# Interleaving the stages of neighbouring channel groups in an FFT convolution that feeds a token-mixing layer

## The chip, the cores and the metric

The kernel runs on one core of one Trainium2 chip. The metric is the device time of one execution in microseconds (us). The kernel before took 2565.59 us (median of 2 runs, 2563.41 to 2567.76). Runs and profiled executions are not the same thing. Times of stages come from one profiled execution of each kernel, whose span is within about 6 us of the median of its runs.

Names of engines in the profile: PE is TensorE (matmuls), PEld its weight loads, which overlap the matmuls (busy 2141.6 and 1267.6 us of a span of 2569.7), DVE is VectorE, ACT is ScalarE, POOL is GpSimd, SP is SyncE, which here only issues transfers. A letter q after an engine (ACTq, SPq) marks the transfers which that engine issues. PSUM is the memory into which this kernel's matmuls write, and VectorE or ScalarE copy the results out of it. The weights of a matmul are the operand whose load the profile shows as an instruction of its own, LDWEIGHTS (stage A of the kernel before has 1280 of them for 1280 matmuls).

## The reference

Two layers in a row. The first convolves each of 128 channels of `x` along the sequence with a filter `h`, by Fourier transforms of twice the length. The second mixes the tokens with two 5696 x 5696 matrices.

```python
x: (8, 5696, 128)    h: (5696, 128)
def _attn_ref(x, h):
    L = 2 * S                                     # 11392
    Yf = np.fft.rfft(x, n=L, axis=1) * np.fft.rfft(h, n=L, axis=0)[None]
    return np.fft.irfft(Yf, n=L, axis=1)[:, :S, :]

def _moe_ref(x, w_theta, w_tok_r, w_tok_i, w_ch):  # x is the convolution's output
    theta = x @ w_theta
    zr, zi = x * np.cos(theta), x * np.sin(theta)
    y = einsum('ts,bsd->btd', w_tok_r, zr) + einsum('ts,bsd->btd', w_tok_i, zi)
    u = x + y
    return u + np.maximum(u @ w_ch, 0.0)
```

## The kernel before

The kernel has four parts, one after another in time: a setup (tables of sines, the spectrum of `h`), the convolution in eight groups (four pairs of batches times two halves of 64 channels), a middle part that loads the convolution's output `yt_hbm`, transposes it into tiles of 128 tokens and forms cosine and sine, and the token mixing.

The transform of length 11392 is split into 178 x 64, and of the 178 row frequencies the 90 from 0 to 89 are computed, in two halves of 45 (`KH`). One group consists of four stages, which I call A, B, C and D.

```python
# A, row transforms: 8 chunks of 8 matmuls for each frequency half
def f1(x16, d0, kh, m):
    a_ = fa.tile([P, 2 * KH, HD], F16, tag="a", name="a_")
    lhs = x16.rearrange("p b n d -> p (b n) d")
    for q in range(0, HD, 8):
        ps = psum()
        for i in range(8):
            nc.tensor.matmul(ps[:m, ...], lhs[:NB, :m, d0 + q + i],      # weights: columns 128 elements apart
                             f1_t[:NB, kh]..., start=True, stop=True)
        nc.scalar.activation(a_[:m, :, q:q + 8]..., ps[:m, ...], AF.Copy)
    return a_
...
for bp in range(B // 2):
    x16 = load_x(lambda e: x[2 * bp + e], 2)
    for dh in range(2):
        for kh in range(2):
            a_ = f1(x16, dh * HD, kh, P)
            for c, (c0, ck) in enumerate(CHK):       # B: 6 chunks per half
                hs = fh.tile([P, 2, HD * CK], F16, tag="hs", name="hs")     # 3 buffers
                nc.sync.dma_start(hs, hf_hbm[dh, kh * NCK + c])
                ps = f2(a_, kh, c, 2)
                xs = fs.tile(...)
                nc.scalar.activation(xs..., ps..., AF.Copy)
                k0 = kh * KH + c0
                for r in range(2):                   # the product with the spectrum
                    nc.vector.tensor_tensor(uv[r][:, :, :, k0:k0 + ck], xs..., hv..., op=mult)
        for q in range(0, 2 * HD, 8):                # C: 16 chunks of 16 matmuls
            ps = psum()
            for i in range(8):
                nc.tensor.matmul(o, u_t[:, at:at + P], r_u, start=True, stop=False)
                nc.tensor.matmul(o, v_t[:, at:at + P], r_v, start=False, stop=True)
            # copied out of PSUM by VectorE for a third of the chunks, by ScalarE for the others
        for n0, cn in CHN:                           # D: 7 chunks
            et = fs.tile([P, CN, 2, NB], F16, tag="et", name="et")          # 2 buffers
            nc.sync.dma_start(et[:K1, :cn], e_hbm[:, n0:n0 + cn, :, :])
            ... matmuls on g_ and et ...
            nc.vector.tensor_copy(yt[...], ps[...])
        for e in range(2):
            nc.sync.dma_start(yt_hbm[dh * HD:(dh + 1) * HD, 2 * bp + e, :], yt[...])
```

In the middle part, ScalarE issues the loads of `ya` in 17 pieces, and all 45 token tiles are transposed and stored there, though the mixing needs only the first 22 at its start.

```python
for p_ in [0, 1, 2, 4, 5, 6, 3, 7] + list(range(8, len(pieces))):        # 17 pieces
    nc.scalar.dma_start(ya[:, :, t0:t1], yt_hbm[:, :, t0:t1])
...
        y_ap = rows_of(ti)            # transpose, copy, store: a tile that is needed now
        phases_b(ti, y_ap, ...)       # its cosine and sine
        if rest:
            rows_of(rest.pop())       # and one of the late tiles 22..44
```

## Time and profile before

The time of the profiled execution (span 2569.7 us) falls into these parts. The bounds are the first matmul of stage C, the issue of the last store of `yt_hbm`, and the first matmul of the mixing.

| part | from – to (us) | length |
|---|---|---|
| setup, and A and B of the first group | 0 – 164.2 | 164.2 |
| groups, from the first C to the last D | 164.2 – 738.8 | 574.6 |
| middle | 738.8 – 907.6 | 168.8 |
| mixing | 907.6 – 2569.7 | 1662.1 |

The head of the page of the kernel before gives the busy time of each engine over the whole span, with its share and number of instructions. Two rows of its part with 40 slices follow (each about 64 us; tenths of the slice in which TensorE was busy, and tenths of full clock that TensorE was granted).

```profile
span 2569.7 us, 42694 instructions
PE 2141.6 (83%) x16395; PEld 1267.6 (49%) x16567; DVE 1729.4 (67%) x2942; ACT 728.2 (28%) x988; POOL 814.1 (32%) x1507
PE   4375776757645569999999999979999999999998
PEclk9975666666668679999999999999999999999998
```

The 83% is an average of two different programs. Counted from zero, the slices from 15 on show TensorE nearly full at full clock (one of them has a 7). In slices 3 to 11, where the groups run, it is busy for four to seven tenths, at a clock of five to six tenths. The views of windows show the same by part. Each line gives the window, its length, busy time and number of instructions for PE, PEld, DVE, ACT and POOL, then the mean granted clock, the busy share of the transfer engines and GB/s. (The profile counts a packet whole in the window in which it starts, so a share can come out a little above 1.) The lines are the setup, one whole group (432 to 504), the middle, and the mixing once it is at its pace.

```profile
core 0: us, PE busy (x) PEld busy (x) DVE busy (x) ACT busy (x) POOL busy (x), PEclk, DMA share, GB/s
0.00:164.20 164.20, 76.36 (x1104) 74.76 (x1105) 88.77 (x105) 92.93 (x124) 18.03 (x31) 0.93 0.42 104
432.00:504.00 72.00, 51.65 (x879) 50.16 (x880) 40.74 (x37) 34.43 (x39) 0.00 (x0) 0.67 0.35 94
738.80:907.60 168.80, 79.13 (x788) 61.95 (x800) 81.88 (x111) 89.69 (x110) 0.00 (x0) 0.70 0.84 234
977.00:2570.00 1593.00, 1549.74 (x7815) 734.94 (x7969) 1212.12 (x2368) 270.73 (x446) 759.80 (x1408) 0.99 0.83 149
```

In the group of 72 us no engine is busy for more than 52 us, and the transfers take a third of their time. The stages mostly follow one another, each with another limit. The trace of the same group shows that the first products (from 443.57 us) wait 10.20 us for ScalarE, which copies stage A out as TensorE delivers it. It also shows two durations for one product of the same shape, 0.69 us in the first frequency half and about 1.3 us in the second. The columns are start, duration, engine, line, operation, operands, and in brackets the idle time before it with what ended it.

```profile
443.57 0.69 DVE L255 TENSOR_TENSOR u_t<-xs,hs 128x1024 f16<-128x1024 f16 x1 [10.20 <-ACT xs L250]
460.41 1.28 DVE L255 TENSOR_TENSOR u_t<-xs,hs 128x1024 f16<-128x1024 f16 x1 [2.08 <-ACT xs L250]
```

In the middle part, the trace of ScalarE shows it issuing 17 loads for 35.22 us before its first copy of a transposed tile at 782.34 us.

```profile
747.07 35.22 ACTq L416 DMA_DIRECT2D ya<-yt_hbm  x17
782.34 0.60 ACT L429 ACTIVATE y_ap<-tpz 128x512 bf16<-128x512 bf16 x1 [64.22 <-issue]
```

The page's part with the costliest groups of instructions gives the two lines that the argument returns to: all products into `u_t` (96 of them, the mean of the two durations), and the weight loads of stage A, which the profile books at 263 ns each.

```profile
L255 DVE TENSOR_TENSOR u_t<-xs,hs 128x1024 f16<-128x1024 f16 x96 | 127.8, 1332 | 130.0 <-ACT xs L250 95.3
L189 PEld LDWEIGHTS <-x 89*128 89x128 f16 (+1 forms) x1280 | 157.3, 263 | 78.4 <-issue 64.9
```

The mean of 1332 ns in the first line is above both 0.69 and 1.3 us. The reason is a third kind of product. The kernel before computes stage A of the second half beside stage B of the first, and there some products take longer still, like this one, while TensorE runs matmuls of A:

```profile
450.02 3.37 DVE L255 TENSOR_TENSOR v_t<-xs,hs 128x1024 f16<-128x1024 f16 x1
450.36 3.05 PE L189 MATMUL ps<-f_t,x 89*128 89x90 f16 x24 [1.23 <-ACT xs L250]
```

Sorted by this overlap, the trace is clear. Of the 80 products of this shape in the first halves, the 38 that ran beside matmuls of A for 0.3 us or more took 1.05 to 4.55 us, and all but one of the others 0.66 to 0.72 (that one overlapped for 0.23 us and took 0.73). ScalarE's copies of A don't do it: the 8 smaller products (128x640) of these halves that ran beside such copies and beside no matmul of A took 0.84 to 0.91 us (those of the second halves, beside neither, 0.89 to 0.94), and those beside matmuls of A 1.17 to 2.70. GpSimd is not busy in the group shown (0.00 us).

So the order of a group in the kernel before is A0, B0 with A1 beside it, B1, C, D.

### The profile page before, as it was taken

The page shows a single profiled execution, that of the slowest core. Times are in us where ns is not written, and L with a number is a line of the kernel's source. Part 1 is how long each engine was busy: PE and PEld are TensorE (multiplying, and loading weights), DVE is VectorE, ACT ScalarE, POOL GpSimd, SP SyncE. Part 2 cuts the span into 40 slices and gives each one's busy share as a digit, 9 for nine tenths or more (in the row PEclk, how much of TensorE's full clock was granted, in tenths as well). Part 3 has the DMA queues.
Part 4 walks back from the last instruction along what each step waited for, and adds up shares of the span by engine and source line. Part 5 has one row for each costly group of instructions (what it writes and reads, how often), then busy time and mean ns, then how long its engine had stood idle before and what let it go on. Part 6 is the DMA issues. An engine that isn't in the chain of part 4 may idle for free.

```text
span 2569.7 us, 42694 instructions
## 1 busy us (share of the span) xinstructions
PE 2141.6 (83%) x16395; PEld 1267.6 (49%) x16567; DVE 1729.4 (67%) x2942; ACT 728.2 (28%) x988; POOL 814.1 (32%) x1507
## 2 busy tenths in 40 slices
PE   4375776757645569999999999979999999999998
PEld 4365676657634434444444444433444444444444
DVE  6355554555514668888878876769777777777774
ACT  6454453445417622333323310000111111111111
POOL 1000000000020014445554565534445544454441
PEclk9975666666668679999999999999999999999998
DMA  1725344343388778889978999897788877888773
GB/s 34 178 82 131 105 108 108 97 103 99 93 190 231 220 219 160 164 166 168 159 142 158 162 163 151 136 260 125 137 140 153 142 138 136 140 153 137 141 134 67
DMA packets 399093, 367.99 MB, mean 143 GB/s; under 512 B 58400, under 2 KB 340170, under 8 KB 397062
## 3 DMA queue, kind: packets, MB, share of 16 engines
q0 software_dynamic: 218240, 143.00, 41.4%
q1 hardware_dynamic: 156951, 197.86, 26.4%
q10 hardware_dynamic: 23696, 24.38, 3.1%
q8 instruction: 130, 2.13, 0.3%
q14 instruction: 76, 0.62, 0.1%
HBM read 404.85 MB, written 103.12 MB: 198 GB/s over the span
## 4 chain that ended last, share of the span: by engine, by line
PE 61%; DMA 10%; DVE 6%; issue 4%; ACT 3%; POOL 1%; ACTq 1%; SPq 0%; DVEq 0%; POOLq 0%
PE m L741 49%; DMA et<-e_hbm 2%; PE ps L265 2%; PE ps L264 2%; DVE v_t L255 2%; DMA hs<-hf_hbm 2%; PE ps L189 2%; DMA y_hbm<-y_ap 2%; DMA wb<-in_moe_w_tok_r_dram 1%; ACTq L416 1%; POOL wb L466 1%; PE ps L281 1%; DVE c L748 1%; DVE u_t L255 1%; DMA wb<-in_moe_w_tok_i_dram 1%
## 5 line engine op out<-in xcount | busy, mean ns | idle before, releaser
L466 POOL DMA_DIRECT2D wb<-in_moe_w_tok_i_dram x720 | 387.8, 547 | 899.0 <-DVE wt L475 809.3
L466 POOL DMA_DIRECT2D wb<-in_moe_w_tok_r_dram x720 | 386.7, 548 | 296.5 <-ACT g__9038 L271 186.8
L741 PE MATMUL m<-b,wt 128*128 128x512 bf16 x1891 | 451.3, 382 | 20.8 <-DVE b L391 9.8
L475 DVE STREAM_TRANSPOSE wt<-wb 128x384 f32<-128x384 f32 (+2 forms) x720 | 359.9, 524 | 125.1 <-PE m L741 69.4
L741 PEld LDWEIGHTS <-wt 128*128 128x128 bf16 x1936 | 190.0, 98 | 252.0 <-issue 20.2
L748 DVE TENSOR_TENSOR c<-c,m 128x512 f32<-128x512 f32 x440 | 283.6, 669 | 0.0
L557 ACT ACTIVATE uts<-utp 128x512 bf16<-128x512 bf16 (+1 forms) x90 | 53.3, 592 | 615.9 <-PE utp L555 615.9
L264 PE MATMUL ps<-r_u,u_t 128*128 128x128 f16 x1024 | 133.3, 235 | 111.7 <-DVE u_t L255 111.7
L189 PE MATMUL ps<-f_t,x 89*128 89x90 f16 (+1 forms) x1280 | 160.7, 324 | 76.5 <-ACT xs L250 18.6
L255 DVE TENSOR_TENSOR u_t<-xs,hs 128x1024 f16<-128x1024 f16 x96 | 127.8, 1332 | 130.0 <-ACT xs L250 95.3
L189 PEld LDWEIGHTS <-x 89*128 89x128 f16 (+1 forms) x1280 | 157.3, 263 | 78.4 <-issue 64.9
L264 PEld LDWEIGHTS <-u_t 128*128 128x128 f16 x1024 | 107.5, 106 | 112.9 <-DVE u_t L255 112.9
L250 ACT ACTIVATE xs<-ps 128x1024 f16<-128x1024 f32 x96 | 108.8, 1151 | 113.9 <-DVE v_t L255 88.0
L108 POOL DMA_DIRECT2D x<-in_x_dram x16 | 8.6, 544 | 407.5 <-PE ps L189 407.5
L265 PE MATMUL ps<-r_v,v_t 128*128 128x128 f16 x1024 | 129.6, 234 | 0.8
L255 DVE TENSOR_TENSOR v_t<-xs,hs 128x1024 f16<-128x1024 f16 x96 | 122.4, 1275 | 0.0
L552 ACT ACTIVATE ub<-c 128x512 bf16<-128x512 f32 (+1 forms) x90 | 56.5, 628 | 222.3 <-DMA wb<-in_moe_w_tok_i_dram 158.6
L206 PEld LDWEIGHTS <-w_t 64*128 64x128 f16 x3240 | 96.4, 126 | 32.0 <-issue 29.8
L283 DVE CAST yt<-ps 128x890 bf16<-128x890 f32 (+1 forms) x56 | 55.5, 1004 | 80.5 <-PE ps L281 80.2
L265 PEld LDWEIGHTS <-v_t 128*128 128x128 f16 x1024 | 107.8, 106 | 2.9 <-DVE v_t L255 2.9
L423 PE MATMUL tpz<-ident_bf,ya 128*128 128x128 bf16 (+1 forms) x360 | 34.8, 260 | 68.5 <-DMA ya<-yt_hbm 39.5
L309 ACT ACTIVATE yT<-tpz 128x512 bf16<-128x512 bf16 x46 | 27.1, 590 | 179.5 <-PE tpz L305 179.5
(2851 smaller groups left out, 3830.6 us busy)
## 6 DMA issues: line engine op xcount, KB each, us to landing
wb<-in_moe_w_tok_r_dram POOLq DMA_DIRECT2D x352, 96.0 KB, 4.5
wb<-in_moe_w_tok_i_dram POOLq DMA_DIRECT2D x352, 96.0 KB, 4.8
wb<-in_moe_w_tok_r_dram POOLq DMA_DIRECT2D x352, 80.0 KB, 4.5
wb<-in_moe_w_tok_i_dram POOLq DMA_DIRECT2D x352, 80.0 KB, 3.7
hs<-hf_hbm SPq DMA_DIRECT2D x96, 256.0 KB, 2.6
cp_hbm<-c SPq DMA_DIRECT2D x88, 256.0 KB, 2.4
c<-cp_hbm SPq DMA_DIRECT2D x88, 256.0 KB, 4.4
out_dram<-c SPq DMA_DIRECT2D x88, 256.0 KB, 4.2
```

What stands on the lines that cost most here:

```text
L189: nc.tensor.matmul(ps[:m, i // 4, (i % 4) * 2 * KH:(i % 4 + 1) * 2 * KH], lhs[:NB, :m, d0 + q + i], f1_t[:NB, kh].rearrange("p r k -> p (r ...
L206: nc.tensor.matmul(ps[:, e, j * HD:(j + 1) * HD], w_t2[rows, k1, N2 * (1 - ri):N2 * (3 - ri)], a_[rows, ri * KH + c0 + j, :], start=(ri == ...
L250: nc.scalar.activation(xs[:, :, :, :ck], ps[:, :, :ck * HD].rearrange("p e (k d) -> p e d k", k=ck), AF.Copy)
L255: nc.vector.tensor_tensor(uv[r][:, :, :, k0:k0 + ck], xs[:, :, :, :ck], hv[:, r:r + 1, :, :ck].to_broadcast([P, 2, HD, ck]), op=mult)
L264: nc.tensor.matmul(o, u_t[:, at:at + P], r_u, start=True, stop=False)
L265: nc.tensor.matmul(o, v_t[:, at:at + P], r_v, start=False, stop=True)
L283: nc.vector.tensor_copy(yt[:, :, n0:n0 + cn].rearrange("p m (a q) -> p m a q", q=nq), ps[:, :cn // nq, :nq * NB].rearrange("p a (q m) -> p ...
L466: nc.gpsimd.dma_start(wb[32 * i:32 * i + 32, :ng, :nj * 64], bass.AP(tensor=a.tensor, offset=a.offset + row0 * S + p * H + i * QR + j0 * 6 ...
L475: nc.vector.transpose(wt.rearrange("p j t r -> p (j t r)").bitcast(F32).rearrange("p (j g t) -> p g j t", j=TJ, g=4)[:, :ng, :nj], wb[:, : ...
L552: nc.scalar.activation(ub[:m].rearrange("p b d -> p (b d)"), c[:m], AF.Copy)
L741: nc.tensor.matmul(ms[q], a[q][:, j, :, r], bts[jj][q][:, r, :], start=(jj == 0 and r == 0), stop=(jj == NJ - 1 and r == 1 and q not in left))
L748: nc.vector.tensor_tensor(c, z, ms[q], op=op)
```

## The change

The change has four parts, meant to fill the idle engines of the first three parts of the span. It leaves the arithmetic of the mixing alone.

1. **Order.** Each stage becomes a list of steps. Stage C of a group is put in program order between the steps of stage A of the next group, and stage D between those of the next stage B.
2. **Even halves.** The 90 frequencies are split into 46 and 44 instead of 45 and 45, so that the second half starts at an even column. All copies of stage C out of PSUM go to VectorE, those of D to ScalarE.
3. **Setup.** The spectrum of `h` is computed for both channel halves in one pass, with both halves of the array's rows in use, and stored in 16 transfers at its end. A chunk of the tables takes two sines and a change of sign instead of three sines. `h` has a buffer of its own, so that the first `x` is loaded at the start.
4. **Late tiles.** The middle loads and transposes only the 22 tiles that the mixing needs first (8 loads instead of 17). The 23 late tiles are loaded, transposed and stored during the mixing, among work of that kind that was there before. With it, the mixing loads some addends later than before.

```diff
+    HALF = ((0, K1 // 2 + 1), (K1 // 2 + 1, K1 // 2 - 1))
...
-        h16 = load_x(lambda e: h, 1)
+        x16s = {0: load_x(0)}
...
-        for dh in range(2):
-            for kh in range(2):
-                a_ = f1(h16, dh * HD, kh, 64)
-                for c, (c0, ck) in enumerate(CHK):
-                    ps = f2(a_, kh, c, 1)
-                    nc.scalar.activation(hst[:, kh * NCK + c, :, :ck], ps[...], AF.Copy, scale=16.0 / NF)
-            ... stores of this half
+        for kh in range(2):
+            for step in stage_a(lambda q: h16[...][:, :, q], kh, a_h):
+                step()
+        for c, (kh, c0, ck) in enumerate(CHK):
+            ps = f2(a_h, c)
+            ... copied by VectorE and ScalarE in turn
+        for dh in range(2):
+            for kh in range(2):
+                for ri in range(2):
+                    for e in range(2):
+                        (nc.sync if e else nc.scalar).dma_start(hf_hbm[dh, ...], hst[kh][...])
...
-                    if q % 24 == 8:
-                        nc.vector.tensor_copy(g_out, g_in)
-                    else:
-                        nc.scalar.activation(g_out, g_in, AF.Copy)
+                nc.vector.tensor_copy(st["g"][...], ps[...])
...
+        def woven(*lists):
+            steps = [((i + 0.5) / len(l), n, f) for n, l in enumerate(lists) for i, f in enumerate(l)]
+            for _, _, f in sorted(steps, key=lambda s: s[:2]):
+                f()
...
+        a0, a_of = front(0)
+        woven(a0)
+        woven(stage_b(a_of, 0))
+        setup.close()
+        for g, (bp, dh) in enumerate(groups):
+            st = {}
+            nxt, a_of = front(g + 1) if g + 1 < len(groups) else ([], None)
+            woven(stage_c(st), nxt)
+            if dh == 0 and bp + 1 < B // 2:
+                x16s[bp + 1] = load_x(bp + 1)
+            woven(stage_b(a_of, groups[g + 1][1]) if nxt else [], stage_d(st, bp, dh))
...
-        ya = sbc.tile([P, B, S], BF16)
-        for p_ in [0, 1, 2, 4, 5, 6, 3, 7] + list(range(8, len(pieces))):
-            nc.scalar.dma_start(ya[:, :, t0:t1], yt_hbm[:, :, t0:t1])
+        ya = sbc.tile([P, B, H], BF16)
+        for p_ in (0, 2, 4, 6, 1, 3, 5, 7):
+            nc.scalar.dma_start(ya[:, :, p_ * PW:p_ * PW + PW], yt_hbm[:, :, p_ * PW:p_ * PW + PW])
...
-                if rest:
-                    rows_of(rest.pop())
...
             def first():
+                tpz = mps.tile([P, 4, P], BF16, tag="misc", name="tpz")
+                for b in range(4):
+                    nc.tensor.transpose(tpz[:m, b, :], st["yT"][:, b, :m], ident_bf)
...
```

## The prediction

> **What bounds it now** (windows by stage, chain of waits, timeline). The 2570 us span has four stages. Setup and the first group up to its products: 0-164. Eight channel groups, one after another: 164-739. Load, transpose, phases, until the first mixing matmul: 739-907. Mixing: 907-2570, where TensorE is 97% busy after about 977; the change adds nothing for TensorE there. All gain must come from the first three stages, where no engine is bound: in a typical group (432-504, 72 us) TensorE is busy 51.6, VectorE 40.7, ScalarE 34.4 us, at a granted clock of 0.67. The stages A (row matmuls, 16 us), B (frequency matmuls and product), C (inverse, 256 matmuls), D (second inverse) run in turn, each limited by another resource: A by TensorE, B by VectorE and the loads of the spectrum (waits of 4.4 us, 15.6 us where x loads as well), C by TensorE while ScalarE waits, D by loads of its table (9 us of waits).
>
> **What changes, costed**
> 1. Even halves. The product takes 0.69 us in half 0 and 1.30 us in half 1, whose first column, 45, is odd. [...] With halves 46 and 44 all take 0.69: about 7 us per group less VectorE work. All C evictions go to VectorE (16 x 1.22 = 19.5 us, 13 more), D's to ScalarE. New sums: VectorE about 35, ScalarE about 31 us per group.
> 2. Interleaving. C runs beside the next group's A, B beside D. C+A: C is 256 x 54 ns at full clock (107 at half) and A 128 x 0.115 us, limited by weight loads at either clock. That is 29 us warm, 43 cold, plus 3.5 us of drain. [...] this trace shows 0.5 in A and D, 1.0 in C. I expect mostly full: 36 us. B+D: ScalarE 18, TensorE 18-21, DMA about 5 MB at 280 GB/s with a third prefetched: 24 us, plus 9 where x loads (three times).
>    Loop: 7 x 60 + 27 + 22 (last C) + 14 (last D) = 483 us against 575.
> 3. Setup. One spectrum pass (360 paired matmuls instead of 720 half-width operations, 12 evictions on two engines instead of 24 on one), two sines per table chunk instead of three, x loaded at the start (TensorE waited 16.7 us for it). But table stores queue behind spectrum stores. First products done at about 108 instead of 164.
> 4. Middle. 8 load pieces instead of 17, so ScalarE stops issuing after about 15 us, not 35; 23 transposed tiles (46 evictions, 6 MB of stores, waits up to 7.8 us for them) leave it. What is left is 22 tiles x 3.6 us on ScalarE: about 100 us against 168.
> 5. Mixing. 46 small stores and 256-byte loads are added; TensorE work is equal. +5 us.
>
> **Sum**: 2566 - 56 - 92 - 60 + 5 = about 2363 us. Range 2300 to 2440. Chances: faster 0.96, same 0.03, slower 0.01.
>
> **What would show it**: (1) products all near 0.69 us; (2) C+A near 36 and B+D near 24 us with granted clock 0.8 or more; (3) the first C matmul near 108 us; (4) about 100 us from the last inverse store to the first mixing matmul; (5) mixing 1660-1670 us.
>
> **What would make it wrong**: a clock that stays at half in C+A (+14 us a group, about 100 us); spectrum and table loads in B+D limited by DMA; store order in the setup holding the tables; late-tile loads starving mixing at its start.

Two statements are cut from this text, where a cut is marked. "All take 0.69" and "mostly full" are estimates. The trace of the kernel before shows 0.69 us for a product of the half that starts at column 0 and 1.28 us for one of the half that starts at 45. Its granted clock was 0.50 in an A (436 to 440 us) and late in D (495 to 504), and 1.00 in most of C (478 to 486) and early in D (487 to 491). A matmul of C follows the one before it after 107 ns at the clock of 0.50 (473 to 476 us), and after about 55 ns at 1.00 (477 to 478). Those of A take 126 ns at either: 40 in 5.03 us from 144.05, at 0.50, and 32 in 4.02 us from 128.65, at 1.00. The 0.115 us of the text is the author's estimate; "warm" and "cold" there mean the full and the half clock. The 280 GB/s are near the 282 that the transfers moved from 740 to 780 us, at a share of 1.05.

## The result, and the profile after

The changed kernel took 2366.57 us (median of 2 runs, 2365.2 to 2367.94), and its output is correct. Ratios in this text are the mean time of one kernel's runs over that of the other's runs in the same rounds, so they are not quite the ratios of the medians. Here the ratio is 0.9224 (95% interval 0.9184 to 0.9265). The same kernel was run once more as a control in the last round of experiments: 2366.09 us, ratio 0.9229 (0.9215 to 0.9243).

| part | before (us) | after (us) | difference | predicted difference |
|---|---|---|---|---|
| setup, to the first C | 164.2 | 128.6 | −35.6 | −56 |
| groups | 574.6 | 474.6 | −100.0 | −92 |
| middle | 168.8 | 101.2 | −67.6 | −60 |
| mixing | 1662.1 | 1659.0 | −3.1 | +5 |
| whole span | 2569.7 | 2363.4 | −206.3 | −203 |

The head and the same two rows of the slices of the kernel after:

```profile
span 2363.4 us, 42201 instructions
PE 2068.5 (88%) x16255; PEld 1184.1 (50%) x16255; DVE 1671.0 (71%) x2943; ACT 641.9 (27%) x895; POOL 841.2 (36%) x1527
PE   3367868686567999999999999799999999999997
PEclk9578879788789999999999999999999999999998
```

TensorE lost only 73 us of busy time (2141.6 to 2068.5), while the span lost 206. The rest is idle time that went. In the groups (slices 3 to 9 here, of 59 us each) TensorE is busy for six to eight tenths at a clock of seven to nine, and it is full from slice 13 on. The windows by part show how. The lines are, in this order, the setup, a C+A phase, a B+D phase in which the next `x` is loaded, the next C+A, a B+D without a load of `x`, the last D, the middle, and the mixing at its pace.

```profile
0.00:128.60 128.60, 45.95 (x976) 43.50 (x976) 77.62 (x99) 71.38 (x86) 44.81 (x51) 0.74 0.54 132
128.60:162.00 33.40, 33.34 (x446) 33.01 (x448) 20.54 (x17) 13.14 (x17) 1.31 (x3) 0.94 0.08 22
162.00:198.00 36.00, 13.71 (x437) 12.46 (x431) 14.36 (x24) 15.63 (x19) 0.84 (x2) 0.71 0.95 216
198.00:232.00 34.00, 33.96 (x458) 33.62 (x459) 19.71 (x18) 13.29 (x18) 0.00 (x0) 0.91 0.19 56
232.00:257.00 25.00, 15.89 (x438) 14.31 (x431) 15.08 (x24) 15.58 (x18) 0.00 (x0) 0.70 0.82 228
581.50:603.00 21.50, 10.58 (x122) 8.89 (x119) 5.45 (x13) 6.14 (x8) 13.45 (x26) 0.50 1.13 186
603.20:704.40 101.20, 55.97 (x614) 41.48 (x614) 65.43 (x81) 73.40 (x83) 0.00 (x0) 0.87 0.92 264
713.00:2363.40 1650.40, 1599.37 (x8148) 751.32 (x8146) 1255.46 (x2446) 286.11 (x468) 771.72 (x1430) 0.99 0.85 155
```

A group now takes 33.4 + 36.0 or 34.0 + 25.0 us instead of 72. In C+A TensorE is busy all the time at a clock above 0.9, and the transfers are nearly idle (share 0.08 and 0.19). In B+D it is the other way round: the transfers are at 0.95 with `x` and at 0.82 without, and all engines wait. So the change turned a loop without a bound into two phases: one that TensorE fills, and one in which everything mostly waits for transfers. The last window shows the mixing at the same pace as before (0.99 of the clock, TensorE 97% busy).

The products now take the short time, with one exception: the longest of the 96 into `u_t` took 0.696 us and the longest into `v_t` 0.689, except for the last one of a group. That one is of 512 elements; in four of the eight groups it runs into the first matmuls of the next A and takes 1.09 to 1.15 us, in the others 0.43 to 0.45. In the page's costliest groups, their line halved from 1332 to 660 ns (the mean contains smaller shapes). What ends VectorE's waits before them is now the load of the spectrum `hs`. The weight loads of stage A are as long as before.

```profile
L274 DVE TENSOR_TENSOR u_t<-xs,hs 128x1024 f16<-128x1024 f16 x96 | 63.4, 660 | 116.1 <-DMA hs<-hf_hbm 88.2
L189 PEld LDWEIGHTS <-x 89*128 89x128 f16 x1024 | 137.1, 269 | 36.6 <-issue 36.5
```

In the setup, ScalarE stands for 16.14 us with nothing computed, put down by the trace to a transfer of the spectrum from `v_t`, and SyncE issues the seven stores of the table `et` only from 78.78 us, over 28.03 us. The first product comes at 112.27 us and the first matmul of C at 128.62.

```profile
74.60 1.05 ACT L161 ACTIVATE et<-whole,half_pi 90x890 f16<-90x890 f32 x1 [16.14 <-DMA hf_hbm<-v_t]
78.78 28.03 SPq L260 DMA_DIRECT2D e_hbm<-et  x7
112.27 0.69 DVE L274 TENSOR_TENSOR u_t<-xs,hs 128x1024 f16<-128x1024 f16 x1 [8.84 <-ACT xs L271]
128.62 0.29 PE L287 MATMUL ps<-r_u,u_t 128*128 128x128 f16 x1 [5.61 <-DVE u_t L274]
```

In the middle, ScalarE is through with its 8 issues after 14.56 us:

```profile
611.11 14.56 ACTq L460 DMA_DIRECT2D ya<-yt_hbm  x8
625.71 0.60 ACT L473 ACTIVATE y_ap<-tpz 128x512 bf16<-128x512 bf16 x1 [22.80 <-issue]
```

### The profile page after: what moved, and what is told of

It reads as the page before. It is cut to its first block, busy times and chain, and to the rows that moved or that the text cites. A ratio compares the mean times of both kernels' runs of the same rounds, so it can differ in the third digit from the quotient of the medians.

```text
span 2363.4 us, 42201 instructions
## 1 busy us (share of the span) xinstructions
PE 2068.5 (88%) x16255; PEld 1184.1 (50%) x16255; DVE 1671.0 (71%) x2943; ACT 641.9 (27%) x895; POOL 841.2 (36%) x1527
## 4 chain that ended last, share of the span: by engine, by line
PE 60%; DMA 4%; DVE 4%; issue 2%; POOL 2%; ACT 2%; ACTq 1%; SPq 0%; DVEq 0%; POOLq 0%
PE m L784 55%; DMA wb<-in_moe_w_tok_r_dram 2%; POOL wb L506 1%; DMA wb<-in_moe_w_tok_i_dram 1%; DVE c L791 1%; PE v L603 1%; PE utp L596 1%; PE m L745 1%; PE m L747 1%; PE m L788 1%; DVE wt L515 1%; ACTq L460 1%; DMA b<-zr_hbm 1%; PE theta_ps L367 0%; PE tpz L545 0%
## 5 line engine op out<-in xcount | busy, mean ns | idle before, releaser
L189 PE MATMUL ps<-f_t,x 89*128 89x88 f16 (+1 forms) x1024 | 145.4, 302 | 36.1 <-ACT a__864 L191 31.6
L189 PEld LDWEIGHTS <-x 89*128 89x128 f16 x1024 | 137.1, 269 | 36.6 <-issue 36.5
L274 DVE TENSOR_TENSOR u_t<-xs,hs 128x1024 f16<-128x1024 f16 x96 | 63.4, 660 | 116.1 <-DMA hs<-hf_hbm 88.2
L288 PE MATMUL ps<-r_v,v_t 128*128 128x128 f16 x1024 | 140.4, 231 | 0.3
L271 ACT ACTIVATE xs<-ps 128x1024 f16<-128x1024 f32 x96 | 91.7, 975 | 32.6 <-DVE v_t L274 29.0
L547 ACT ACTIVATE yb<-tpz 128x512 bf16<-128x512 bf16 (+1 forms) x46 | 27.4, 597 | 184.5 <-PE tpz L545 132.3
L208 PEld LDWEIGHTS <-w_t 64*128 64x128 f16 x3240 | 63.7, 105 | 17.6 <-issue 12.5
L307 ACT ACTIVATE yt<-ps 128x890 bf16<-128x890 f32 (+1 forms) x56 | 48.0, 858 | 78.9 <-PE ps L305 78.9
L605 DVE SCALAR_TENSOR_TENSOR c<-v,c 128x512 f32<-128x512 f32 (+1 forms) x90 | 61.6, 684 | 11.0 <-PE v L603 10.5
L369 ACT ACTIVATE red<-theta_ps,magic 128x512 f32<-128x512 f32 (+1 forms) x46 | 31.6, 687 | 129.0 <-PE theta_ps L367 100.0
```

The lines of the kernel that those rows point to most:

```text
L189: nc.tensor.matmul(ps[:, i // 4, (i % 4) * 2 * kn:(i % 4 + 1) * 2 * kn], lhs(q + i), f1_t[:NB, 2 * k0:2 * k0 + 2 * kn], start=True, stop=True)
L208: nc.tensor.matmul(ps[:, e, j * HD:(j + 1) * HD], w_t2[rows, k0 + c0 + j, N2 * (1 - ri):N2 * (3 - ri)], a_[rows, ri * kn + c0 + j, :], sta ...
L271: nc.scalar.activation(xs[:, :, :, :ck], ps, AF.Copy)
L274: nc.vector.tensor_tensor(uv[r][:, :, :, k0:k0 + ck], xs[:, :, :, :ck], hv[:, r:r + 1, :, :ck].to_broadcast([P, 2, HD, ck]), op=mult)
L605: nc.vector.scalar_tensor_tensor(c[:m], v[:m], 0.0, c[:m], op0=ALU.max, op1=ALU.add)
```

## The experiments

The total was as predicted, but not its terms: the setup gave 20 us less, and the three other parts together 24 us more. Three questions follow. Which part of the change made the loop faster, the order or the even halves? What holds each of the new phases? And why did the setup fall short? The theory about the loop was that the order is nearly all of it; its rival was that the cheaper products and the moved copies give a good part by themselves. For the B+D phase with `x` the theory was that the 3 MB of a load of `x` compete with the spectrum for transfer time; the rival was that the three buffers of `hs` are too few. For C+A the theory was that the weight loads of A, which read columns 256 bytes apart, hold TensorE; the rival was that C's copies on VectorE (16 times 1.22 us = 19.5 us) do. For the setup the theory was that ScalarE and SyncE wait in their own queues of stores; the rival was that the bytes of the spectrum are the limit, whoever issues them.

Twelve kernels ran. The kernel before ran with medians of 2564.05, 2563.75 and 2564.13 us. "Change" is the median less that of the control (2366.09). The last four columns are the parts of the profiled execution, cut as above.

| kernel | median us | ratio to before (95%) | change | setup | groups | middle | mixing |
|---|---|---|---|---|---|---|---|
| c_after (control) | 2366.09 | 0.9229 (0.9215–0.9243) | 0 | 127.5 | 470.4 | 101.5 | 1665.5 |
| e1_seq | 2463.78 | 0.9606 (0.959–0.9623) | +97.7 | 127.6 | 570.4 | 101.7 | 1662.4 |
| e2_odd | 2390.84 | 0.9329 (0.9301–0.9357) | +24.8 | 133.3 | 490.8 | 101.9 | 1661.8 |
| e9_seq_odd | 2500.81 | 0.9749 (0.973–0.9768) | +134.7 | 132.1 | 600.8 | 101.3 | 1660.6 |
| e3_oldlate | 2429.45 | 0.9474 (0.9457–0.949) | +63.4 | 128.0 | 471.8 | 163.4 | 1663.5 |
| e5_setup | 2361.61 | 0.9206 (0.9187–0.9224) | −4.5 | 119.5 | 472.5 | 101.4 | 1663.6 |
| e11_half (wrong output) | 2354.32 | 0.9182 (0.9169–0.9196) | −11.8 | 111.6 | 477.8 | 102.2 | 1662.1 |
| e6_hs | 2348.79 | 0.9157 (0.9139–0.9175) | −17.3 | 125.8 | 457.6 | 101.2 | 1667.3 |
| e7_nox (wrong output) | 2324.88 | 0.9056 (0.9035–0.9076) | −41.2 | 127.3 | 429.1 | 101.1 | 1668.0 |
| e8_contig (wrong output) | 2292.82 | 0.8936 (0.8921–0.895) | −73.3 | 122.3 | 404.3 | 101.2 | 1662.7 |
| e10_early | 2336.93 | 0.9117 (0.9102–0.9132) | −29.2 | 129.2 | 445.5 | 101.3 | 1663.5 |
| e12_best | 2294.10 | 0.8948 (0.8933–0.8964) | −72.0 | 118.7 | 408.9 | 104.4 | 1663.2 |

The control shows how far two profiled executions of one kernel differ: 4 us in the groups (470.4 and 474.6) and 6.5 us in the mixing (1665.5 and 1659.0). Differences of that size in one part mean nothing.

### c_after: the control

The changed kernel, unedited, ran beside the last three experiments.

> The changed kernel again, unedited, as the control for this call's chip: 2362 to 2370 us, ratio to the kernel before 0.922. A difference of more than 5 us from its first measurement would put the small differences of the earlier calls in doubt.

It gave 2366.09 us, against 2366.57 in the first comparison.

### e1_seq: one stage after another, with everything else of the change

```diff
-            woven(stage_c(st), nxt)
+            woven(stage_c(st))
+            woven(stage_d(st, bp, dh))
+            woven(nxt)
             if dh == 0 and bp + 1 < B // 2:
                 x16s[bp + 1] = load_x(bp + 1)
-            woven(stage_b(a_of, groups[g + 1][1]) if nxt else [], stage_d(st, bp, dh))
+            woven(stage_b(a_of, groups[g + 1][1]) if nxt else [])
```

> Undoes only the interleaving: program order C, D, A, B of each group again; even halves, evictions, setup and late part as in the changed kernel. Theory O (overlap of stages with different limits is what took 100 us out of the eight groups): C alone is then bound by its VectorE evictions (16 x 1.22 = 19.5 us, plus 3), D about 12, A 16, B about 16, so about 66 us a group instead of 57 to 71: the groups take 530 to 550 us instead of 474, total 2420 to 2445 us. Rival V (less VectorE work by even halves and moved evictions is what counts): total below 2390 us.

The kernel lost 97.7 us, and its groups took 570.4 us, against 470.4 in the control and 574.6 in the kernel before. With the stages one after another, the rest of the change in the loop is worth 4 us in all, which is within the spread of the control; so the gain of the groups is there only together with the interleaving. (The 4 us are the difference of two larger effects, see e9_seq_odd.) The text expected 530 to 550 us for the groups in this order, so the order is worth more than it said. One reservation: this is stricter than the order of the kernel before, which had A1 beside B0. What the even halves would give in exactly that order was not run. The windows of one group of this run show its stages A, B, C and D by themselves.

```profile
400.00:416.00 16.00, 16.00 (x162) 15.92 (x163) 0.00 (x0) 12.45 (x17) 0.00 (x0) 0.50 0.42 129
416.00:434.00 18.00, 7.70 (x334) 6.92 (x329) 14.30 (x24) 11.53 (x12) 0.00 (x0) 0.69 0.51 147
434.00:454.00 20.00, 17.56 (x256) 17.02 (x254) 17.28 (x17) 0.00 (x0) 0.00 (x0) 0.86 0.10 30
454.00:470.00 16.00, 10.31 (x137) 9.53 (x138) 1.21 (x2) 5.95 (x7) 0.00 (x0) 0.58 0.38 104
```

A and C take 36 us apart and 33 to 34 together; B and D take 34 apart and 25 or less together, where no `x` loads. So C+A saves 2 to 3 us of the 70 shown, and B+D 9 or more. The larger part of the gain comes from B+D, whose stages apart leave TensorE idle for 36 to 57% of their time and the transfers for about half of it or more.

A second thing is in the first line. TensorE is busy for all of the 16 us of A, and yet it is granted half the clock, in each cut of 3 us from 400 to 415 us and again at the start of the next A (469 to 475). Interleaved with C it has 0.91 to 0.95. But A gains little from the higher clock, as the small saving in C+A shows, and as the kernel before does with its 126 ns for a matmul of A at a clock of 0.50 and of 1.00; e8 tells why.

### e2_odd and e9_seq_odd: the odd halves, in the new order and in the old

```diff
-    HALF = ((0, K1 // 2 + 1), (K1 // 2 + 1, K1 // 2 - 1))
+    HALF = ((0, K1 // 2), (K1 // 2, K1 // 2))
```

> Undoes only the even halves (45 and 45 again). The products of half 1 go from 0.69 to 1.30 us, 7 us more VectorE work per group. Theory O: in B+D ScalarE (18 us) and the spectrum loads end last, VectorE rises from 15 to 22 us and is nearly hidden: 0 to 3 us a group, total 2366 to 2390 us. Rival V: all 7 us of each of eight groups show, total about 2420 us.

> Both undone: order C, D, A, B and halves 45 and 45. Against the run with only the order undone, theory O expects that the even halves are worth more here, because B stands alone and its second half is bound by VectorE (as in the kernel before): 4 to 7 us a group, 32 to 56 us. Theory V expects the same difference in both orders.

The odd halves cost 24.8 us in the new order (e2 against the control) and 37.0 us in the old one (e9 against e1), or 3.1 and 4.6 us for each of the eight groups. Interleaving hides a part of what the even halves save, but less of it than I had expected. The trace of e2_odd shows the two durations side by side. The lines are a product of the first half (an even start column) and one of the second (start column 45):

```profile
189.30 0.69 DVE L274 TENSOR_TENSOR v_t<-xs,hs 128x1024 f16<-128x1024 f16 x1
195.91 1.32 DVE L274 TENSOR_TENSOR v_t<-xs,hs 128x1024 f16<-128x1024 f16 x1
```

Shape, types and sources are the same, and the destination's start differs by 2 bytes modulo 4. The groups of e9_seq_odd took 600.8 us, 26 more than those of the kernel before, though both have odd halves and neither interleaves C and D. Two things differ between their loops: C's copies are all on VectorE and D's on ScalarE, and A1 is no longer beside B0. No run tells them apart, but the traces do. From the first matmul of C to the first of D, each group of e9_seq_odd takes 21.1 to 21.8 us, and each of the kernel before 17.3 to 18.6; over the eight groups this is 26.7 us. From the last matmul of D to the first C of the next group (A and B) the two take 309 and 311 us in sum over seven groups. So the 26 us are C's, which now waits for 16 copies of 1.22 us on one engine, and the overlap of A1 and B0 in the kernel before had gained nothing. It follows for e1_seq that with the stages in turn the moved copies cost some 26 us and the rest of the change gave back about 30. Whether the moved copies cost anything in the new order, where VectorE is busy for 20 of 33 us in C+A, was not run. The longest product of e9_seq_odd took 1.33 us, so the products of up to 4.55 us in the kernel before went with the overlap of A1 and B0.

### e3_oldlate: the late tiles back in the middle

The convolution is that of the kernel after, and everything that follows it is that of the kernel before: 17 loads, 45 tiles transposed in the middle, and the addends loaded as before.

```diff
-        ya = sbc.tile([P, B, H], BF16)
+        ya = sbc.tile([P, B, S], BF16)
...
+                if rest:
+                    rows_of(rest.pop())
...
```

> The changed convolution with the old late part (17 load pieces, 23 tiles transposed in front of the mixing). If the late part's gain is its own: 60 to 70 us between the last inverse store and the first mixing matmul come back and the mixing stays within 5 us, total 2425 to 2440 us. If the saving was only moved into the mixing (rival: pushed-back work costs there), total below 2400 us.

The kernel lost 63.4 us. Its middle took 163.4 us against 101.5 in the control, and its mixing 1663.5 against 1665.5. So the saving in the middle is not paid back in the mixing, where the late tiles run among matmuls that bound it. The prediction's +5 us there isn't seen; it would be within the spread of the control.

### e5_setup: other queues for the setup's stores

```diff
-                        (nc.sync if e else nc.scalar).dma_start(hf_hbm[...], hst[...])
+                        (nc.sync if e else nc.gpsimd).dma_start(hf_hbm[...], hst[...])
...
-            nc.sync.dma_start(e_hbm[:, n0:n0 + cn, :, :], et[:K1, :cn, :, :])
+            nc.gpsimd.dma_start(e_hbm[:, n0:n0 + cn, :, :], et[:K1, :cn, :, :])
```

> The changed kernel with the spectrum stores that ScalarE issued and the table stores that SyncE issued put on GpSimd's queue. Theory Q (what the prediction missed in the setup is queueing: ScalarE stands 16 us, 58.5 to 74.6, in its own spectrum stores, and the table stores wait behind spectrum loads): the first inverse matmul comes at 110 to 118 us instead of 128.6, total 2350 to 2358 us. Rival B (8.4 MB of stores in that stretch are bound by the DMA engines): it moves by less than 5 us.

The first product came at 89.94 us instead of 112.27, the first matmul of C at 119.5 instead of 127.5 to 128.6, and the whole kernel gained only 4.5 us. (The runs of the two kernels don't overlap, but the intervals of their ratios do, so the 4.5 us are barely clear of the noise; the 8 to 9 us at the first C are a difference of single traces.) This lies between the two theories: ScalarE is free, but then VectorE waits 25.30 us for the spectrum to come back, as the line of its first product shows.

```profile
89.94 0.69 DVE L274 TENSOR_TENSOR u_t<-xs,hs 128x1024 f16<-128x1024 f16 x1 [25.30 <-DMA hs<-hf_hbm]
```

The reason is in the kernel after as well. This is a stretch of its setup in which no engine computes anything and the transfers run full:

```profile
66.00:72.00 6.00, 0.00 (x0) 0.00 (x0) 0.00 (x0) 0.00 (x0) 0.00 (x0) 0.50 1.02 281
```

From 57 to 84 us the share is 1.01 over the whole stretch, while the 16 stores of 384 KB (6.3 MB) land. In e5_setup TensorE and ScalarE work in the same 66 to 72 us (6.00 and 5.52 us busy), so it was the order of issue that stopped these two, and not the full transfers.

### e11_half: half of the spectrum's bytes, on top of e5 (wrong output on purpose)

```diff
-        for dh in range(2):
+        for dh in range(1):
             for kh in range(2): ... stores of hf_hbm[dh]
...
-                nc.sync.dma_start(hs, hf_hbm[dh, c])
+                nc.sync.dma_start(hs, hf_hbm[0, c])
```

> Wrong result on purpose: the kernel with the setup's stores moved to GpSimd's queue, and only the first half of the spectrum (3.1 instead of 6.3 MB) is stored, read by all groups. Theory B (the bytes stored before the first spectrum load lands hold the setup: DMA share 1.0 from 60 to 84 us): the first product comes at 75 to 82 us instead of 89.9 and the first inverse matmul at 105 to 112 instead of 119.5, total 8 to 15 us below that kernel. If the order of work on VectorE and ScalarE (tables built between the products) holds it: less than 4 us.

The second channel half is computed and not stored, and the groups read the first one instead, so the output is wrong while the amount of work in the groups is the same. Against e5_setup the first C came 7.9 us earlier (111.6) and the kernel gained 7.3 us. That is a little under what the text gives for it, and the first product, at 85.5 us, came later than it says. So the setup's shortfall has two parts of about the same size: about 8 to 9 us because the stores stand in the queues of ScalarE and SyncE (e5, which moves both and doesn't separate them), and about 8 us because of half of the bytes (e11). Together they are 16 to 17 of the 20 us. What the rest is stays open; the other half of the bytes, which no run took away, is a candidate.

### e6_hs: eight buffers for the spectrum instead of three

```diff
-        fh = pool("fft_h", 3)
+        fh = pool("fft_h", 8)
```

> The changed kernel with 8 instead of 3 buffers for the spectrum chunks. Theory P (in B+D the loads of spectrum and table end last, while the DMA engines are nearly idle, 0.08 to 0.2, in C+A, because only three chunks can be fetched ahead): five more chunks, 1.3 MB, are fetched in C+A, each B+D loses 3 to 5 us, total 2330 to 2350 us. Rival T (the table loads, two buffers, hold B+D by themselves): less than 10 us.

The kernel gained 17.3 us; of the 13.0 us between its trace and that of the control, 12.8 are in the groups. Measured from the last matmul of A or C to the first of the next C, the B+D phases without `x` took 21.1 us in the mean against 22.9 in the control, and the ones with `x` 35.6 against 37.9. So each phase lost about 2 us, less than the 3 to 5 that were expected. The ones with `x` are still much the longer, with the transfers as full as before (this window ends 2 us after the next C has begun):

```profile
159.80:196.00 36.20, 16.26 (x452) 14.81 (x442) 14.47 (x25) 15.32 (x18) 0.74 (x2) 0.68 0.95 214
```

The list of waits of that phase says what took over. Its columns are engine and line, what it waited for, us in total, how often, and the longest. These two of its lines are from the kernel after, for its phase from 162.2 to 198 us:

```profile
DVE u_t L274 <- DMA hs<-hf_hbm: 21.0, 6, 16.5
PE ps L305 <- DMA et<-e_hbm: 17.3, 3, 11.1
```

And this is from e6_hs, for 159.8 to 196 us:

```profile
DVE u_t L274 <- ACT xs L271: 21.1, 7, 11.5
PE ps L305 <- DMA et<-e_hbm: 18.7, 3, 11.0
```

The spectrum is there in time, and the 11 us for one load of the table `et`, of which there are two buffers, are unchanged. As B and D are interleaved in program order, TensorE runs no matmul of B either while it waits these 11 us in D. The buffers of `hs` were a limit of 2 us a phase, but they are not what makes the phases with `x` 14 us longer than the others.

### e7_nox: no further loads of x (wrong output on purpose)

```diff
-                x16s[bp + 1] = load_x(bp + 1)
+                x16s[bp + 1] = x16s[0]
```

> Wrong result on purpose: x is loaded for the first pair only and used again. B+D takes 36 to 38 us where x loads and 22 to 25 where not. If the x load is what does it, the three long phases fall to 22 to 25 us: total about 2325 us (2320 to 2332). If something else differs in those phases, less than 15 us.

The kernel gained 41.2 us, or 14 us for each of the three loads left out, and the phases that had held them fell to 22 to 25 us, like the others. So it is the bytes of `x` that stretch these phases from some 24 to 36 us. The prediction had allowed 9.

### e10_early: stage A in the first quarter of C, so that x loads during C+A

If the bytes of `x` are the cause, they can be moved to where the transfers are idle. Stage A of the next group is the last reader of the buffer of `x`, so A must be finished early for the load to start early.

```diff
-        def woven(*lists):
-            steps = [((i + 0.5) / len(l), n, f) ...
+        def woven(*lists, rush=1.0):
+            steps = [((i + 0.5) / len(l) * (rush if n else 1.0), n, f) ...
...
-            woven(stage_c(st), nxt)
+            woven(stage_c(st), nxt, rush=0.25 if dh == 0 and bp + 1 < B // 2 else 1.0)
```

> Only the weave of the three C+A phases before an x load is changed: A's chunks go into the first quarter of C, so that the x buffer comes free earlier and x loads while the DMA engines are idle. Theory D (the long B+D phases are bound by the bytes of x, spectrum, table and result together, DMA share 0.95): B+D falls from 36 to 23 to 26 us in those three groups, C+A grows by 2 to 4 us as VectorE's evictions then end last, total 25 to 35 us less than the control. Rival L (B+D is long for the latency of its own loads, not for x's bytes): less than 10 us.

The kernel gained 29.2 us with a correct output. The windows show a C+A phase with the load in it, and the B+D phase that follows:

```profile
128.60:165.00 36.40, 33.62 (x400) 33.14 (x400) 20.30 (x18) 11.87 (x16) 2.16 (x4) 0.67 0.45 97
165.00:190.00 25.00, 15.47 (x457) 13.99 (x458) 14.92 (x25) 15.76 (x18) 0.00 (x0) 0.74 0.75 202
```

The transfers' share rose from 0.08 to 0.45 in C+A, and B+D fell from 36.0 to 25.0 us. It has a price: C+A became 3 us longer (33.4 to 36.4), at a clock of 0.67 instead of 0.94. Cut finer, the clock is 0.50 from 129 to 147 us, where A is crowded with a few chunks of C, and 1.00 from 153 us on, where C is alone; TensorE is busy throughout both.

### e8_contig: stage A with contiguous weights (wrong output on purpose)

```diff
-                return x16.rearrange("p b n d -> p (b n) d")[:NB, :, dh * HD + q]
+                at = (dh * HD + q) * P
+                return x16.rearrange("p b n d -> p (b n d)")[:NB, at:at + P]
```

> Wrong result on purpose: A reads its weights as 128 neighbouring columns instead of every 128th. C+A takes 33 us with TensorE busy throughout: an A chunk of 8 takes about 1.0 us, a C chunk 0.87. Theory W (A is held by loading weights with a stride of 256 bytes, whatever the clock): A chunks fall to 0.5 to 0.6 us, C+A becomes bound by VectorE's evictions (16 x 1.22), 22 to 25 us, total 2295 to 2320 us. Rival K (A is held by its own matmuls at the granted clock): less than 10 us.

The weights of A have the same number of columns and bytes, but they lie next to one another instead of 256 bytes apart. The kernel gained 73.3 us. The first C+A phase took 22.10 us instead of 33.40:

```profile
124.00:146.10 22.10, 21.58 (x416) 21.42 (x415) 19.46 (x16) 13.24 (x17) 1.44 (x3) 0.92 0.09 19
```

The groups of instructions of this phase, first the weight loads of A in the kernel after (129 to 162 us), busy time and mean ns after the bar:

```profile
L189 PEld LDWEIGHTS <-x 89*128 89x128 f16 x126 | 17.2, 269 | 0.0
```

and in e8_contig (124 to 146 us), with the copies of C below:

```profile
L189 PEld LDWEIGHTS <-x 89*128 89x128 f16 x122 | 6.5, 102 | 0.0
L289 DVE CAST g__1475<-ps 90x1024 f16<-90x1024 f32 x16 | 19.5, 1221 | 3.3 <-PE ps L288 3.3
```

The strided weight load takes 2.6 times as long as the contiguous one, and it set the length of the phase. By what mechanism, no run shows; shown is only the dependence on the stride. A's matmuls are busy for 8.0 us (122 of them) instead of 18.5 (128), or 0.52 us for eight, as the text expected. With the stride gone, TensorE is busy for 21.58 and VectorE for 19.46 of the 22.10 us: the rival, C's copies, is at most the next limit, and not the present one. The stride also explains the slow products. In both kernels the last product of a group can run into the first matmuls of the next A, here with strided weights (the kernel after) and with contiguous ones (e8_contig):

```profile
128.46 1.14 DVE L274 TENSOR_TENSOR v_t<-xs,hs 128x512 f16<-128x512 f16 x1
122.10 0.44 DVE L274 TENSOR_TENSOR v_t<-xs,hs 128x512 f16<-128x512 f16 x1
```

Four such products in the kernel after took 1.09 to 1.15 us (seven in e7_nox 1.12 to 1.15), and seven in e8_contig 0.43 to 0.45. So it is strided weight loads on TensorE that slow a product of VectorE beside them; by what mechanism, no run shows.

A kernel with a correct output would have to bring `x` into the other layout first. That was not tried, and its cost is open.

### e12_best: the correct edits together

e5's queues, e10's early A, five buffers of `hs` instead of e6's eight, and four buffers for the table `et` in a pool of its own.

```diff
-        fh = pool("fft_h", 3)
+        fh = pool("fft_h", 5)
...
+        fe = pool("fft_e", 4, side="right")
...
-                et = fs.tile([P, CN, 2, NB], F16, tag="et", name="et")
+                et = fe.tile([P, CN, 2, NB], F16, tag="et", name="et")
... and the edits of e5_setup and e10_early
```

> A version meant to beat both: setup stores on GpSimd's queue, five spectrum and four table buffers instead of three and two, and A in the first quarter of C where an x load follows. If the three gains add (5, 15 to 20 and 25 to 33 us): 45 to 55 us below the control, total 2310 to 2322 us. If the early x load and the deeper prefetch compete for the same idle DMA time: 30 to 40 us.

The output is correct, and the time is 2294.10 us (2291.8 to 2298.66, 5 runs), 0.8948 of the kernel before and 72.0 us under the control. The three single edits add up to 51.0 us (4.5 + 17.3 + 29.2). The remaining 21 us, which the text did not expect, come from their combination, or from the four buffers of `et`, which no run tried alone. The traces say a part of it. In the last D no `x` and no spectrum is loaded, so of all these edits only the buffers of `et` reach it: from first to last matmul it took 12.5 us, against 19.9 in the control and 21.1 in e6_hs, and TensorE's waits for `et` there fell from 10.2 to 3.2 us. That is some 7 of the 21. The four B+D phases without `x` fell to 19.4 us in the mean (last matmul of A or C to the next C), against 21.1 in e6_hs and 23.5 in e10_early, which fits the same cause. The rest isn't separated. This version beats both kernels.

## Why the prediction was right, and where its terms were off

The predicted time was 2363 us (2300 to 2440), and 2366.57 was measured. The direction, the parts and the mechanisms held. The closeness of the total is partly luck: the terms were off by +20.4 (setup), −8.0 (groups), −7.6 (middle) and −8.1 us (mixing), which is −3.3 us in sum. Within the groups it is the same: the seven C+A phases took 20 us less than predicted, the seven B+D phases 5 more and the last D 7.5 more.

- **"All gain must come from the first three stages"** held. The mixing went from 1662.1 to 1659.0 us, while its start moved from 907.6 to 704.4.
- **Even halves, "all take 0.69"** held: the median product of the kernel after is 693 ns. The exception is the product beside strided weight loads (e8_contig), which the prediction didn't know. It gave the even halves no time of their own on the critical path, only less work on VectorE (7 us a group). e2_odd shows that 3.1 us a group of it reach the time. There the product with an even start column took 0.69 us and the one with an odd start column 1.32 us; whether anything but an even or odd start counts, no run shows.
- **C+A, 36 us,** was measured as 32.3 to 34.0, with a clock of 0.91 to 0.95 as hoped; that is near its figure for the full clock (29 + 3.5). The danger named, a half clock in C+A, did not come. The clock was 0.50 in A alone (e1_seq) and where A is crowded (e10_early), and above 0.9 where A and C alternate. But the first 32 matmuls of A in the kernel before, also alone, ran at 1.00 (108.9 to 113 us). What sets the clock, no run shows. The limit by A's weight loads, which the prediction named ("128 x 0.115 us, limited by weight loads at either clock"), was confirmed by e8_contig (269 ns for a weight load with the stride, 102 without).
- **B+D, 24 us,** was measured as 21.3 to 25.0. The predicted clock of 0.8 or more was seen there only in part (0.70 to 0.84), and it probably did not matter, as the waits of the phase are for transfers (share 0.82); no run tests this.
- **"plus 9 where x loads (three times)"** was too small. Those phases took 36 to 36.5 us, some 13 more than the others, and without the loads the kernel gains 14 us for each (e7_nox).
- **"14 (last D)"** was too small: 21.5 us. GpSimd's loads of the mixing's weights begin at the end of the last C and bring the transfers to a share of 1.13. This was to be read before: in the kernel before the last D took 21.3 us (717.5 to 738.8) at a share of 0.98, while the D of an earlier group took 16.5 (487.5 to 504). With four buffers of `et` the last D was short again (e12_best).
- **Middle, "about 100 us against 168"** held: 101.2 against 168.8. The sum nevertheless counted only 60 for it, and the prediction gives no reason. e3_oldlate shows that the saving is not moved elsewhere.
- **Setup, −56, is the term that failed.** The step was "First products done at about 108 instead of 164". They were done at 128.6. The prediction did say "But table stores queue behind spectrum stores", and listed the order of stores among the things that could make it wrong, but gave it no time. The one-pass spectrum saves the work of TensorE as expected (76.36 us busy in the old setup, 45.95 in the new), but it also moves all 16 stores to one point, at which the engines that issue them and those that need the spectrum wait: 6.3 MB, 27 us at a share of 1.01. In their place the runs showed two costs of about 8 us each, the stores in the queues of engines that should compute (e5_setup) and the bytes themselves (e11_half), and about 4 us that remain open. The 35.6 us that the setup did gain rest on its two traces; no run undoes this part alone.
- **Mixing, +5,** was not seen, and is below what two executions of one kernel differ by.

## What to carry to other kernels

Where the stages of a loop have different limits and neither is full over the loop, put stages with complementary needs side by side in program order: here undoing it cost 98 of the 199 us that were gained, while undoing the cheaper products cost 25. Which stages are put together matters: the kernel before had A beside B, where it gained nothing: A's weight loads slowed B's products there (from 0.66 to 0.72 us to 1.05 to 4.55). Then look again at what each new phase is bound by, because here the phase that is full of matmuls had room for transfers (a share of 0.08 to 0.20) and the neighbouring one had not (0.81 to 0.95); moving one load across that border was worth another 29 us. And when a sum of terms is checked against a result, check it term by term: this one was 3 us off in all and 20 us off in its setup, because stores that used to be spread out had been gathered to one point and were given no time.
